# Lightning attention and SwiGLU on one core: the loads of two groups moved ahead of two transposes in the load queue

## The chip, the cores and the metric

The kernel runs on one core of a Trainium2 chip. The metric is device microseconds of one execution, from the chip's own clock. Beside it stands one execution taken by the hardware profiler, whose span runs from the first to the last instruction of the program.

## The reference

Linear attention with a decay per head is followed by a gated feed-forward layer. Inputs q, k and v have batch 4, 8 heads, 768 positions and 64 columns; everything is float32.

```python
for b in range(nb):                      # blocks of 64 positions
    intra = einsum('bhic,bhjc->bhij', qb, kb) * Dmask          # lam ** (i - j), i >= j
    intra = einsum('bhij,bhjd->bhid', intra, vb)
    inter = einsum('bhid,bhde->bhie', qb * lam_pow, kv_state)
    out[:, :, sl] = intra + inter
    kv_state = lam_block * kv_state + einsum('bhsd,bhse->bhde', kb * rev_pow, vb)
x = out.transpose(0, 2, 1, 3).reshape(3072, 512)
g = x @ w_gate                           # 512 x 1536
y = (g * sigmoid(g) * (x @ w_val)) @ w_out                     # 1536 x 512
```

## The kernel before

The 3072 rows are cut into 12 groups of 256 positions of one batch row, numbered 0 to 11. Two groups make one tile of the feed-forward layer, so there are six tiles, t = 0 to 5. The ninth and the tenth group have the numbers 8 and 9, and form tile 4.

Each group goes through the same stations:

- `load_group` (L255) issues its loads on SP's queue, through `load_fp32` (L101). From group 6 on (`NAT0`), k and q are each loaded in four pieces of 64 partitions (128 KB each), and v in two pieces of 128 partitions (256 KB each): ten DMA issues, L114, 1.5 MB.
- `cast_scaled` (L267) converts k to bf16 on ScalarE (L270), scales q on VectorE (L272) and then calls `dma_transpose` (L260), which issues one transposing DMA (L263) from the tile `qk` to the tile `qkt`, again on SP's queue. It waits for both conversions. In what follows, T6 is the transpose of group 6, and so on.
- `v_scale` (L247) writes the decayed v, on GpSimd or, for group 7, on VectorE.
- `attend` (L696) is the attention of group g and the start of group g + 1: the product of q with the state (`core_a`, L475), the state update's products of g + 1 (`upd_mm`, L396), its scores (`scores_n`, L364, the first to read `qkt` of g + 1), and then the product with v of group g (`core_b`, L488).

The feed-forward part of a tile runs over 12 columns of 128 (`ffn_fc`): four gate products (L530), Silu on ScalarE (L534), four value products (L546), and their product h on VectorE (L549). The output product of tiles 0 and 1 is `ffn_out` (L565), which copies to `osb` on ScalarE (L567) and stores through ScalarE's queue (L568). Later tiles use `out_units` (L639), with sums and differences of h made by `h_combo` (L611).

Nothing reorders the instructions: the schedule is written by hand. A list of steps, one for each tile and column, is walked at L957 to L971; `at(n, fn, ...)` hangs a call on step n, and calls on one step run in the order in which they were registered. Each engine and each queue executes its instructions in the order in which they are issued. SP's queue carries the loads and the transposes, so a transpose that waits for a conversion holds all loads behind it.

For t = 2 the loop at L931 registers these calls, among others: on step `sn[4]` `cast_scaled(7)` and then `load_group(8)`, on step `sn[8]` `cast_scaled(8)` and then `load_group(9)`. For t = 3 it is `cast_scaled(9)` and `load_group(10)` on `sn[0]`, `cast_scaled(10)` and `load_group(11)` on `sn[6]`. `attend(6)` hangs on step 7 of t = 2, `attend(7)` on its step 10, `attend(8)` on step 4 of t = 3.

The loads' buffers come from a pool of ten (`raw`, for k, q and the weights) and one of four (`v`).

Of the kernel before, what the change touches and what calls it, by code (L numbers as in the profile page):

```python
# [19 lines left out]
@with_exitstack  # L20
def kernel(
    ctx: ExitStack,
    tc: tile.TileContext,
    q: bass.AP,
    k: bass.AP,
    v: bass.AP,
    lam: bass.AP,
    moe_w_gate: bass.AP,
    moe_w_val: bass.AP,
    moe_w_out: bass.AP,  # L30
    out: bass.AP,
):
    nc = tc.nc
    with tc.manual_schedule():
        _body(ctx, tc, nc, q, k, v, lam, moe_w_gate, moe_w_val, moe_w_out, out)


def _body(ctx, tc, nc, q, k, v, lam, moe_w_gate, moe_w_val, moe_w_out, out):
# [9 lines left out]
    NG = NBLK * B // 2  # L48
# [787 lines left out]
    def step(t, fc, b0=0, b1=B):  # L836
        steps.append((t, fc, b0, b1))
        return len(steps) - 1

    def at(n, fn, *a):  # L840
        plan.setdefault(n, []).append((fn, a))
# [83 lines left out]
    for t in range(2, NG // 2):  # L925
        order = [c for j in range(FC // 4) for c in (2 * j, 2 * j + 1, FH + 2 * j, FH + 2 * j + 1)]
        sn = [step(t, fc, 2 if t == 2 and fc < NH else 0) for fc in (range(FC) if t == 2 else order)]
        if t == 2:
            at(sn[4], ahead, 6)
            at(sn[5], v_scale, 7, nc.vector)  # L930
        for j, g in ((4 if t == 2 else 0, 2 * t + 3), (8 if t == 2 else 6, 2 * t + 4)):  # L931
            if g < NG:
                at(sn[j], cast_scaled, g)
                if g + 1 < NG:
                    at(sn[j], load_group, g + 1)
                if g > 7:
                    at(sn[1 + j], v_scale, g, nc.gpsimd)
        if t + 1 < NG // 2:
            at(sn[7 if t == 2 else 4], attend, 2 * t + 2)
            if 2 * t + 4 < NG:  # L940
                at(sn[10], attend, 2 * t + 3)
            else:
                at(sn[9], core_a, 2 * t + 3)
                at(sn[10], core_b, 2 * t + 3)
        for n, o in zip((1, 5, 7, 9) if t == 2 else ({3: 11, 4: 7, 5: 5}[t],), outs):
            at(sn[n], *o)
        if t == 2:
            at(sn[7], h_combo, t, 0)
            at(sn[9], h_combo, t, 1)
            at(sn[10], wo_combo, 3)  # L950
        else:
            at(sn[3], h_combo, t, 0)
            at(sn[7], h_combo, t, 1)
        at(sn[11], h_combo, t, 2)
        outs = [(out_units, t)]
# [47 lines left out]
```

## Time and profile before

| what | value |
| --- | --- |
| median of 3 runs | 223.6 us (223.45 to 225.53) |
| profiled execution | 222.9 us, its span 221.2 us |
| TensorE busy | 215.3 us, 97% of the span |
| VectorE, ScalarE, GpSimd busy | 126.2, 111.6, 87.8 us |
| granted TensorE clock | 1.00 |
| traffic | 28.31 MB read, 6.29 MB written |

The span is divided among the engines by their busy time; they overlap. In the lists of the profile, a row of the timeline has the start, the duration, the engine, the line, the operation and the tiles, and at its end in brackets the idle time before it with what ended it. PE is TensorE, DVE VectorE, ACT ScalarE, POOL GpSimd; a small q after the name (SPq) stands for the queue on which an engine issues its DMAs. A row of the waits names who waited for what, the total in us, how often, and the longest.

### The profile page before, as it was taken

The numbers are of one execution on the slowest core, as the hardware profiler recorded it, in microseconds if no ns is written. First come the engines' busy times: TensorE is split into PE (matmuls) and PEld (weight loads), VectorE is DVE, ScalarE is ACT, GpSimd is POOL, SyncE is SP. The second block draws the span as 40 slices with busy tenths as digits, with TensorE's granted clock in tenths as the row PEclk, the third lists the DMA queues.
The fourth block names the chain that finished last, engine by engine and source line by source line (L and its number), as shares of the span: only waits on it lengthen the run. The fifth ranks groups of instructions, "written<-read, shape, count | busy, mean of one in ns | idle before, by whom it ended". The sixth has DMA issues, their size and how long they took to land.

```text
span 221.2 us, 6418 instructions
## 1 busy us (share of the span) xinstructions
PE 215.3 (97%) x2636; PEld 136.4 (62%) x2636; DVE 126.2 (57%) x227; ACT 111.6 (50%) x235; POOL 87.8 (40%) x131
## 2 busy tenths in 40 slices
PE   8999999999999999999999899999999999999994
PEld 4666455888886556454444446864578444884583
DVE  1674357476763692842487888548663456434650
ACT  6788587655544342546273545335633453333332
POOL 6685746927593040589684635330610000000000
PEclk9999999999999999999999999999999999999999
DMA  6999999999997989498578778645001300022013
GB/s 189 343 341 362 372 358 318 265 271 197 375 280 169 235 235 220 128 242 216 118 196 201 166 160 202 157 153 134 3 1 74 119 3 1 0 89 104 0 47 142
DMA packets 88318, 39.72 MB, mean 180 GB/s; under 512 B 57698, under 2 KB 83938, under 8 KB 88290
## 3 DMA queue, kind: packets, MB, share of 16 engines
q1 hardware_dynamic: 84210, 33.50, 58.1%
q10 hardware_dynamic: 4080, 5.83, 7.2%
q8 instruction: 20, 0.33, 0.6%
q14 instruction: 8, 0.07, 0.1%
HBM read 28.31 MB, written 6.29 MB: 156 GB/s over the span
## 4 chain that ended last, share of the span: by engine, by line
PE 95%; ACT 2%; issue 1%; DVE 1%
PE bank L530 28%; PE bank L546 28%; PE bank L639 17%; PE bank L565 10%; PE bank L488 2%; PE bank L475 2%; PE bank L338 1%; PE bank L301 1%; PE bank L396 1%; PE bank L138 1%; PE bank L364 1%; ACT qkt L303 1%; PE bank L179 1%; DVE h L549 1%; PE bank L173 0%
## 5 line engine op out<-in xcount | busy, mean ns | idle before, releaser
L549 DVE TENSOR_TENSOR h<-sil,bank 128x512 bf16<-128x512 bf16 (+1 forms) x91 | 51.2, 574 | 58.2 <-PE bank L546 34.0
L546 PE MATMUL bank<-xt,wv_sb 128*128 128x512 bf16 (+1 forms) x364 | 77.0, 335 | 0.3 <-DVE h L549 0.3
L530 PE MATMUL bank<-xt,wg_sb 128*128 128x512 bf16 (+1 forms) x364 | 77.2, 335 | 0.0
L534 ACT ACTIVATE sil<-bank 128x512 bf16<-128x512 f32 (+1 forms) x91 | 46.1, 512 | 45.9 <-PE bank L530 41.2
L546 PEld LDWEIGHTS <-wv_sb 128*128 128x128 bf16 x364 | 35.5, 98 | 27.2 <-issue 0.6
L530 PEld LDWEIGHTS <-wg_sb 128*128 128x128 bf16 x364 | 34.3, 98 | 25.1 <-DVE xt L500 0.2
L250 POOL TENSOR_TENSOR v_s<-v,dec 128x1024 bf16<-128x1024 f32 (+1 forms) x14 | 22.0, 1582 | 27.2 <-DMA v<-in_v_dram 27.0
L565 PE MATMUL bank<-wo_sb,h 128*128 128x512 bf16 x96 | 21.9, 379 | 0.0
L639 PEld LDWEIGHTS <-h 128*128 128x128 bf16 x192 | 18.8, 98 | 3.0
L345 DVE TENSOR_TENSOR ssb<-bank,causal 128x512 bf16<-128x512 f32 x24 | 15.5, 684 | 5.1 <-PE bank L338 5.0
L435 POOL TENSOR_TENSOR kvf<-kvs,ups 128x256 f32<-128x256 f32 x8 | 5.8, 727 | 29.2 <-ACT ups L418 26.6
L639 PE MATMUL bank<-wo_sb,h 128*128 128x256 bf16 x144 | 16.9, 273 | 0.0
L565 PEld LDWEIGHTS <-h 128*128 128x128 bf16 x96 | 9.1, 98 | 10.4
L639 PEld LDWEIGHTS <-hs 128*128 128x128 bf16 x144 | 14.1, 98 | 1.7
L500 ACT CAST xt<-bank 128x512 bf16<-128x512 f32 x19 | 11.6, 656 | 3.5 <-PE bank L488 2.6
L567 ACT COPY osb<-bank 128x512 f32<-128x512 f32 x8 | 4.7, 587 | 16.6 <-PE bank L565 16.6
L444 POOL CAST kvn<-kvf 64x256 bf16<-64x256 f32 x24 | 11.5, 478 | 1.5
L435 POOL TENSOR_TENSOR kvf<-kvf,ups 128x256 f32<-128x256 f32 x16 | 11.8, 736 | 0.6
L639 PE MATMUL bank<-wt,hs 128*128 128x256 bf16 x96 | 11.7, 273 | 0.0
L418 ACT COPY ups<-bank 128x256 f32<-128x256 f32 (+1 forms) x24 | 9.5, 451 | 1.5 <-PE bank L396 1.3
L270 ACT CAST qk<-kraw 128x1024 bf16<-128x1024 f32 x9 | 9.4, 1043 | 0.4 <-DMA kraw<-in_k_dram 0.4
L272 DVE TENSOR_TENSOR qk<-qraw,qdn 128x1024 bf16<-128x1024 f32 x6 | 8.0, 1328 | 2.7 <-DMA qraw<-in_q_dram 2.7
(89 smaller groups left out, 216.8 us busy)
## 6 DMA issues: line engine op xcount, KB each, us to landing
out_dram<-osb ACTq DMA_DIRECT2D x20, 256.0 KB, 2.7
v<-in_v_dram SPq DMA_DIRECT2D x18, 256.0 KB, 4.5
woraw<-in_moe_w_out_dram SPq DMA_DIRECT2D x6, 512.0 KB, 6.6
kraw<-in_k_dram SPq DMA_DIRECT2D x24, 128.0 KB, 3.7
qraw<-in_q_dram SPq DMA_DIRECT2D x24, 128.0 KB, 3.6
wraw<-in_moe_w_gate_dram SPq DMA_DIRECT2D x5, 512.0 KB, 7.3
wraw<-in_moe_w_val_dram SPq DMA_DIRECT2D x5, 512.0 KB, 6.6
kraw<-in_k_dram SPq DMA_DIRECT2D x4, 512.0 KB, 6.3
```

The lines of the kernel that those rows point to most:

```text
L250: eng.tensor_tensor(out=st[("vs", g)][:, h0:h1], in0=st[("v", g)][:, h0:h1].rearrange("p h (s d) -> p h s d", s=2), in1=vfac(g, h0, h1), o ...
L345: nc.vector.tensor_tensor(out=ssb[:, h2, 2 * c:2 * c + 2].rearrange("p a s n -> p a (s n)"), in0=sp[(c, h2)].rearrange("p (a x) -> p a x", ...
L418: nc.scalar.copy(out=u[:, 0:n], in_=up[r][:, 0:n])
L435: nc.gpsimd.tensor_tensor(out=o, in0=f, in1=u, op=ALU.add)
L444: nc.gpsimd.tensor_copy(out=o[64 - h2 * 64:128 - h2 * 64], in_=f[h2 * 64:h2 * 64 + 64])
L500: fns[r](out=xt[:, g % 2, :, r].rearrange("p h (m s) -> p h s m", s=2) if g < NAT0 else xt[:, g % 2, :, :, r * M:r * M + M], in_=op[r].rea ...
L530: nc.tensor.matmul(gp[:, 0:N], wg_sb[:, mc, fs], xt[:, b0 // 2:b1 // 2, mc].rearrange("p g b n -> p g (b n)"), start=(mc == 0), stop=(mc = ...
L534: nc.scalar.activation(sil[:, 0:N], gp[:, 0:N], AF.Silu)
L546: nc.tensor.matmul(vp[:, 0:N], wv_sb[:, mc, fs], xt[:, b0 // 2:b1 // 2, mc].rearrange("p g b n -> p g (b n)"), start=(mc == 0), stop=(mc = ...
L549: nc.vector.tensor_tensor(out=h_sb[:, fc % FH, b0:b1].rearrange("p b n -> p (b n)"), in0=sil[:, 0:N], in1=vp[:, 0:N], op=ALU.mult)
L565: nc.tensor.matmul(ps, st[("h", t, fc // FH)][:, fc % FH, b], wo_sb[:, fc, c0:c1], start=(fc == 0), stop=(fc == FC - 1))
L639: nc.tensor.matmul(o, lhs(f), rhs(f), start=(start and f == 0), stop=(f == FH - 1), skip_group_check=True)
```

## The change

The loads of groups 8 and 9 are taken out of the loop and hung on steps of their own in tile t = 2: k and q of group 8 on `sn[1]`, its v on `sn[4]`, k and q of group 9 on `sn[6]`, its v on `sn[8]`. They are registered before the loop, so on one step they come ahead of `cast_scaled`. The condition `g > 8` leaves the loop's own loads to groups 10 and 11.

```diff
         if t == 2:
+            at(sn[1], load_group, 8, "kq")
+            at(sn[4], load_group, 8, "v")
+            at(sn[6], load_group, 9, "kq")
+            at(sn[8], load_group, 9, "v")
             at(sn[4], ahead, 6)
             at(sn[5], v_scale, 7, nc.vector)
         for j, g in ((4 if t == 2 else 0, 2 * t + 3), (8 if t == 2 else 6, 2 * t + 4)):
             if g < NG:
                 at(sn[j], cast_scaled, g)
-                if g + 1 < NG:
+                if g + 1 < NG and g > 8:
                     at(sn[j], load_group, g + 1)
```

On SP's queue the order changes as follows (each load stands for its ten issues); the instructions of all other engines keep their order:

```
before:  T6  v7  T7  kqv8  T8  kqv9  T9  kqv10  T10  kqv11  T11
after:   T6  v7  kqv8  T7  kqv9  T8  T9  kqv10  T10  kqv11  T11
```

## The prediction

> **What bounds the kernel now.** I read the first part of the page, the waits of TensorE, its timeline around the moved loads, then the timeline of SP's queue, where the change is made.
>
> ```profile
> PE 215.3 (97%) x2636; PEld 136.4 (62%) x2636; DVE 126.2 (57%) x227; ACT 111.6 (50%) x235; POOL 87.8 (40%) x131
> ```
>
> TensorE is busy 97% of the span and stands for 95% of the chain that ended last. An earlier load gains only where TensorE itself waits for it, and a wait put in front of TensorE is paid in full. Its waits between 60 and 160 us:
>
> ```profile
> PE bank L364 <- DMA qkt<-qk: 0.5, 1, 0.5
> PE bank L546 <- DVE h L549: 0.3, 1, 0.3
> ```
>
> Both fall in one stretch. Its timeline there, with that of group 7 and of group 8 before it:
>
> ```profile
> 98.03 0.49 PE L396 MATMUL bank<-v_s,qk 64*64 64x64 bf16 x32
> 98.34 0.60 PE L364 MATMUL bank<-qkt 64*64 64x64 bf16 x32
> ...
> 109.92 0.42 PE L396 MATMUL bank<-v_s,qk 64*64 64x64 bf16 x24
> 110.35 0.45 PE L364 MATMUL bank<-qkt 64*64 64x64 bf16 x32
> 110.62 0.46 PE L488 MATMUL bank<-ssb,v_s 64*64 64x64 bf16 x32
> 111.01 1.04 PE L530 MATMUL bank<-xt,wg_sb 128*128 128x512 bf16 x4
> 111.89 1.03 PE L546 MATMUL bank<-xt,wv_sb 128*128 128x512 bf16 x4
> ...
> 121.75 0.42 PE L396 MATMUL bank<-v_s,qk 64*64 64x64 bf16 x24
> 122.67 0.49 PE L364 MATMUL bank<-qkt 64*64 64x64 bf16 x32 [0.50 <-DMA qkt<-qk]
> ...
> 123.37 1.04 PE L530 MATMUL bank<-xt,wg_sb 128*128 128x512 bf16 x4
> 124.69 1.02 PE L546 MATMUL bank<-xt,wv_sb 128*128 128x512 bf16 x4 [0.28 <-DVE h L549]
> ```
>
> The L364 rows are the scores of groups 7 (98.34), 8 (110.35) and 9 (122.67); each needs its group's transpose, T7, T8, T9. Only group 9's is late. SP's queue around them:
>
> ```profile
> 57.47 8.51 SPq L263 DMA_TRANSPOSE qkt<-qk  x1
> ...
> 79.05 2.79 SPq L114 DMA_DIRECT2D qraw<-in_q_dram  x4
> 82.01 3.61 SPq L263 DMA_TRANSPOSE qkt<-qk  x1
> 85.66 1.20 SPq L114 DMA_DIRECT2D v<-in_v_dram  x2
> 92.37 1.57 SPq L263 DMA_TRANSPOSE qkt<-qk  x1
> ```
>
> T6 starts at 82.01, T7 at 92.37. A transpose with nothing in flight ahead takes 1.57 to 1.65 us on the queue (T7 to T11). T6, right behind loads, took 3.61; that of group 5, behind 3 MB of w_out, 8.51. The reader should compare their ends with the last load ahead. The last q piece before T6 was issued at 81.18 and landed 4.70 later, 85.88: T6's issue ended at 85.62. The last w_out piece was issued at 56.80, landed 9.37 later, 66.17: that issue ended at 65.98. T4, issued at 46.51 for 5.79 us, ended at 52.30, and the load ahead of it landed at 52.40. So a transpose stays on SP's queue until about 0.2 us before the loads ahead have landed. It then lands about 2.1 us later (T6 at 87.67, T7 at 96.09).
>
> **What it takes away.** With q of group 9 loaded long before, the vector engine's scaling at L272 (117.47, idle 1.69 before it for that DMA) runs right after the h product that ends at 115.78, takes its 1.23, and T9 starts near 117.2, not 118.83. It lands near 121.0, ahead of 122.2. From L396 to L364 group 8 takes 0.43, group 9 0.92: 0.49 us go. From L530 to L546 it is 0.88 against 1.32: that 0.44 is the vector engine still behind after its wait (busy 3.93 of the 4.00 us from 121 to 125). Both: 0.93. If the vector engine stays behind, 0.49. I take 0.9, since 1.69 us of idle time in front of that backlog disappear. TensorE's other gaps in the stretch are nil, so no gain exceeds this. The 1.05 us that group 10's scaling waited at 129.63 go too, but T10 already lands at 134.71, as its scores begin: nothing.
>
> **What it adds: ten issues ahead of T7.** They can start when the second v piece of group 7 is issued, 86.86; their buffers are free, since the w_out pieces that lay in them were cast by 65.3. Eight k and q issues at 0.65 make 5.2, two v issues at 0.62 make 1.25: 93.3. In the built program each issue also waits for an earlier DMA on the same of eight completion semaphores; the second q piece waits for the first v piece of group 7 (85.66 plus 4.86, which its twin took: 90.5), which makes the end 93.9. T7 itself was ready at 92.3, when the scaling ended, so the issuing alone costs 1.6, and a T7 landing 3.7 later, 97.7, would still beat 98.34. What matters is when the second v piece of group 8 lands. The v of group 7 landed at 91.14 (86.28 plus 4.86); behind it lie 1.57 MB. One k or q piece per 0.65 us is 200 GB/s, the GB/s row of the DMA view shows about 250 where v pieces flow: 6.3 to 7.9 us, and a store of 256 KB issued at 95.03 lies within (0.7 us at the 360 GB/s that the row shows beside stores). That gives 97.4 to 99.7. The shortest landing of a v piece behind its own loads (3.7, group 9) from 93.3 gives 97.0. I take 225 GB/s, the middle: 98.1. T7's issue then ends at 97.9 and lands at 100.0; TensorE waits from 98.34: **1.7 us**, bounds 0.6 (97.0) and 3.2 (99.7). Behind the waiting L364 stand the attention product L488, the output product at 99.19 and all gate and value products, so it is all path.
>
> **Ten issues of group 9 ahead of T8: nothing.** SP is free at 97.9; ten issues with their semaphore waits (the third q piece for T7's landing, the v pieces for k pieces behind it) end near 104, the last landing 4.0 later, 107.8. T8 waits for the scaling that ended at 106.49, 1.7 later now: 108.3, issue end 109.9. The cover is 2.1 us. Were it gone, each us would be paid, since T8 lands at 110.36 (106.62 plus 1.64 plus 2.1) for scores at 110.35. T9 then stands directly behind T8. The loads of group 10 are issued earlier than 120.47, and everything after keeps its order. The stores on ScalarE's queue now wait for landings of v7, v8 and k9 on shared semaphores: 91.1, 98.1 and about 103.5, against their issues at 95.03, 102.60 and 108.64; so the Silu behind them is not held. GpSimd's scaling of v9 (idle 2.75 for its load) starts earlier; nobody waited for it.
>
> **Sum.** Minus 0.9, plus 1.7: plus 0.8. The profiled execution took 222.9 (span 221.2 and 1.7 around it), so 223.7; the median of the runs is 0.7 above that execution, so 224.4. Own range, from plus 0.6 minus 0.93 to plus 3.2 minus 0.49 with the far corner cut: 223.3 to 225.9.
>
> A rule speaks against the stall. The Trainium skill, "DMA: Bandwidth & Descriptors", section "Queues, rings and completion order", says that data descriptors carry no barrier and that a later one may finish before an earlier; its "Rules for kernel authors" add that a transpose beside ordinary DMAs needs nothing. By that T7 would land at 97.7, the stall would be 0 and the time 222.7; the three long issues above show a transpose held behind loads, so I go by them.
>
> **Rivals.**
> 1. *T7 is not held.* It lands 3.7 after 93.9, TensorE waits nowhere, only the gain stays: 223.6 minus 0.9, 222.7. For it: T7, T9, T10 and T11 land in 3.7 to 3.8. Against: those had nothing in flight ahead; the three that had were held. 0.12.
> 2. *Slower: the backlog drains badly.* Place: the load queue between 87 and 99, shared with the stores issued at 86.46 and 95.03. When v8 lands after 99.6, T7 lands after 101.5, the stall passes 3.1 and the net passes 2.2 us, one per cent; at 100.5 it is 4.1 minus 0.9: 226.8. For it: a q piece took 4.70 to land with a store beside it, and all of v7, k8, q8, v8 (2.1 MB) now follow T6 without a pause, while before the transfers were idle from 92 to 93.5. Against: 2.1 MB in the 12 us from 87.5 need only 175 GB/s. 0.16. The Trainium skill, "TensorE: Matmul & The Clock Gate", section "Why this matters for your kernels", warns that idle gaps above about 3 us halve the clock; the 0.50 us gap here left it at 1.00, and no run shows a longer one.
> 3. *The gain does not come.* T9 still follows a late scaling, because the vector engine's list is the limit: plus 1.7, 225.3. For it: the 3.93 busy of 4.00. Against: the 1.69 us wait in front of it. 0.10.
>
> My forecast has 0.62. Over and under one per cent (2.2 us), about what a measurement of this kernel can tell from no change: faster needs more than the 0.93 that TensorE lost, 0.02; slower is rival 2, 0.16; the rest, 0.82, lies within. The range goes from rival 1 to the start of rival 2: 222.6 to 226.1.
>
> **What would show it.** In SP's timeline ten issues stand between 85.7 and about 94, and T7's issue is 3 to 5 us long, ending just before v8 lands. TensorE has one new gap of about 1.7 us before the L364 near 98.3, for qkt, and those at 122.67 and 124.69 are gone. The scaling of groups 9 and 10 waits for no DMA. A T7 issue of 1.6 us would prove the holding wrong; a new gap before the scores of group 8 would prove the cover of T8 wrong; a wait of Silu behind a store would show a path that I priced at nothing.

## The result, and the profile after

The changed kernel is slower. Over 20 executions of each, its median is 228.2 us (225.6 to 230.3) against 223.8 us (222.9 to 226.2); the ratio is 1.015 (95% interval [1.012, 1.019]), about 3.4 us. This ratio and those below are of means, and leave out executions more than 1.5% above their kernel's fastest, so it stands below the 1.019 of the plain medians. The forecast was 224.4 us and no measurable change; what came is the slower rival, at the place that it named. The profiled execution took 229.2 us, its span 227.4 us, 6.2 more than before. It is one of the longer ones of its kernel, and that of before (222.9) one of the shorter, so the 6.2 us taken apart here are more than the usual difference.

From the page: the total, the busy time, and the row of TensorE and of its granted clock in 40 slices of 5.7 us.

```profile
span 227.4 us, 6411 instructions
...
PE 215.8 (95%) x2631; PEld 136.4 (60%) x2636; DVE 124.9 (55%) x227; ACT 111.5 (49%) x235; POOL 87.0 (38%) x131
...
PE   8889999999999999946999999999999999999994
...
PEclk9999999999999999995999999999999999999999
```

TensorE's work is the same; one hole has come, in slices 18 and 19, and the clock halves behind it. Its timeline there and at the next two groups:

```profile
98.45 0.49 PE L396 MATMUL bank<-v_s,qk 64*64 64x64 bf16 x32
103.74 0.64 PE L364 MATMUL bank<-qkt 64*64 64x64 bf16 x32 [4.80 <-DMA qkt<-qk]
...
105.14 4.11 PE L565 MATMUL bank<-wo_sb,h 128*128 128x512 bf16 x11 [0.34 <-issue]
109.09 1.03 PE L530 MATMUL bank<-xt,wg_sb 128*128 128x512 bf16 x4
...
118.19 1.04 PE L530 MATMUL bank<-xt,wg_sb 128*128 128x512 bf16 x4
...
130.01 1.04 PE L530 MATMUL bank<-xt,wg_sb 128*128 128x512 bf16 x4
130.89 0.81 PE L546 MATMUL bank<-xt,wv_sb 128*128 128x512 bf16 x3
```

The same stretch before, behind the scores at 98.34:

```profile
99.19 2.76 PE L565 MATMUL bank<-wo_sb,h 128*128 128x512 bf16 x12
101.78 1.03 PE L530 MATMUL bank<-xt,wg_sb 128*128 128x512 bf16 x4
```

The scores of group 7 wait 4.80 us for T7. The two waits of before, for T9 and for h at group 9, are gone, and the scores of group 8 do not wait. The windows of TensorE give busy time by engine, then the granted clock, the DMA share and the GB/s:

```profile
98.40:103.80 5.40, 0.60 (x65) 0.49 (x56) 0.65 (x1) 1.23 (x3) 4.29 (x9) 0.79 1.06 218
103.80:108.40 4.60, 4.26 (x72) 2.22 (x74) 0.69 (x1) 1.07 (x2) 4.00 (x5) 0.51 0.77 173
```

From about 101.5 to 108.3 the clock is half: the output product at 105.14 takes 4.11 us where it took 2.76. So the 6.2 us of span can be put together from the timelines of both:

| stretch | before | after | difference |
| --- | --- | --- | --- |
| start of L396 ahead of group 7's scores | 98.03 | 98.45 | +0.4 |
| L396 to L364: the wait for T7 | 0.31 | 5.29 | +5.0 |
| L364 of group 7 to the first L530: the half clock | 3.44 | 5.35 | +1.9 |
| first L530 after group 8's scores to that after group 9's | 12.36 | 11.82 | -0.5 |
| that L530 to its L546 | 1.32 | 0.88 | -0.4 |

The rest is -0.1. The gain that was forecast is in the last two rows; the stall was three times the forecast, and a second price came with it. On SP's queue:

```profile
84.13 2.89 SPq L263 DMA_TRANSPOSE qkt<-qk  x1
87.07 1.34 SPq L114 DMA_DIRECT2D v<-in_v_dram  x2
88.52 3.34 SPq L114 DMA_DIRECT2D kraw<-in_k_dram  x4
91.97 3.82 SPq L114 DMA_DIRECT2D qraw<-in_q_dram  x4
95.83 1.54 SPq L114 DMA_DIRECT2D v<-in_v_dram  x2
97.54 4.18 SPq L263 DMA_TRANSPOSE qkt<-qk  x1
...
113.65 12.88 SPq L263 DMA_TRANSPOSE qkt<-qk  x2
```

T7 leaves at 97.54, 5.2 us later than before, and stays 4.18 us, until 101.72; the last v piece of group 8 landed at 101.75. T7's own landing is not recorded; its scores start at 103.74, 2.0 us after its issue. The last row is two transposes and the idle time between them: T8 from 113.65 for 1.61 us, T9 from 124.23 for 2.30 us.

The wait differs between executions. A second profiled execution of the changed kernel, taken beside the experiments (`after_again`), shows where else it can go.

> The changed kernel once more, for a second profile of the same order: T7's issue again between 3 and 4.5 us long, the wait before the scores of group 7 between 2.5 and 5 us, no wait before the scores of groups 8 and 9. If the wait passes about 3 us the clock is halved for some us behind it, otherwise not.

It took 230.4 us (span 228.7). T7's issue was as long as expected, 3.98 us; the waits were not as expected. TensorE waited 1.25 us for T7 at 102.39 and then 2.61 us for T8:

```profile
116.83 0.45 PE L364 MATMUL bank<-qkt 64*64 64x64 bf16 x32 [2.61 <-DMA qkt<-qk]
```

Here T7 started earlier (95.79) and TensorE arrived 2.2 us later, probably because a piece of half clock from 15.7 to 19.1 us, long before the change, had delayed it (3.4 us at half speed are 1.7 us). T8's issue took a clean 1.61 us, from 111.46, and yet it landed only at 116.79, beside a store issued at 112.52.

The clock sorts the 20 executions. A mean clock of 0.992 over 226 us is 3.6 us at half speed, 0.985 is 6.8 us.

| mean granted clock | executions | time, us |
| --- | --- | --- |
| 0.999 | 2 | 225.6, 225.8 |
| 0.990 to 0.992 | 10 | 226.0 to 229.2, median 227.6 |
| 0.984 to 0.985 | 8 | 228.4 to 230.3, median 229.0 |

Of 38 executions of the kernel before, taken beside the experiments, five show 0.992 and all others 0.997 or more. Not every such piece comes from the wait for T7 (`after_again` had one at 15.7 us), but 18 of 20 against five of 38 is the change's doing; the two executions without it lost some 1.9 us (225.7 against 223.8).

### The profile page after: what moved, and what is told of

Same layout as the page of the kernel before. It is cut to its first block, busy times and chain, and to the rows that moved or that the text cites. A ratio compares the mean times of both kernels' runs of the same rounds, so it can differ in the third digit from the quotient of the medians.

```text
span 227.4 us, 6411 instructions
## 1 busy us (share of the span) xinstructions
PE 215.8 (95%) x2631; PEld 136.4 (60%) x2636; DVE 124.9 (55%) x227; ACT 111.5 (49%) x235; POOL 87.0 (38%) x131
## 4 chain that ended last, share of the span: by engine, by line
PE 71%; SPq 8%; DMA 8%; issue 5%; POOL 4%; ACT 1%; DVE 0%; POOLq 0%
PE bank L530 23%; PE bank L546 23%; PE bank L639 16%; SPq L114 3%; SPq L107 3%; PE bank L565 3%; DMA wraw<-in_moe_w_val_dram 3%; DMA qkt<-qk 3%; DMA v<-in_v_dram 2%; SPq L225 2%; PE bank L488 2%; POOL v_s L250 2%; PE bank L475 1%; POOL kvf L435 1%; POOL kvn L444 1%
## 5 line engine op out<-in xcount | busy, mean ns | idle before, releaser
L530 PE MATMUL bank<-xt,wg_sb 128*128 128x512 bf16 (+1 forms) x364 | 77.2, 335 | 0.0
L546 PE MATMUL bank<-xt,wv_sb 128*128 128x512 bf16 (+1 forms) x364 | 77.1, 335 | 0.1
L546 PEld LDWEIGHTS <-wv_sb 128*128 128x128 bf16 x364 | 35.5, 98 | 27.1 <-DVE wv_sb L821 0.6
L530 PEld LDWEIGHTS <-wg_sb 128*128 128x128 bf16 x364 | 34.3, 98 | 25.1 <-DVE xt L500 0.2
L250 POOL TENSOR_TENSOR v_s<-v,dec 128x1024 bf16<-128x1024 f32 (+1 forms) x14 | 21.5, 1542 | 24.9 <-PE bank L565 10.5
L565 PE MATMUL bank<-wo_sb,h 128*128 128x512 bf16 x91 | 23.0, 400 | 0.5 <-issue 0.3
L639 PEld LDWEIGHTS <-h 128*128 128x128 bf16 x192 | 18.8, 98 | 3.0
L565 PEld LDWEIGHTS <-h 128*128 128x128 bf16 x96 | 9.6, 103 | 11.7 <-issue 2.4
L444 POOL CAST kvn<-kvf 64x256 bf16<-64x256 f32 x24 | 12.4, 516 | 1.5
L369 DVE TENSOR_TENSOR ssb<-bank,causaln 128x512 bf16<-128x512 f32 x12 | 8.2, 686 | 5.8 <-PE bank L364 5.7
```

Of the source, the lines that this page charges most:

```text
L250: eng.tensor_tensor(out=st[("vs", g)][:, h0:h1], in0=st[("v", g)][:, h0:h1].rearrange("p h (s d) -> p h s d", s=2), in1=vfac(g, h0, h1), o ...
L444: nc.gpsimd.tensor_copy(out=o[64 - h2 * 64:128 - h2 * 64], in_=f[h2 * 64:h2 * 64 + 64])
L530: nc.tensor.matmul(gp[:, 0:N], wg_sb[:, mc, fs], xt[:, b0 // 2:b1 // 2, mc].rearrange("p g b n -> p g (b n)"), start=(mc == 0), stop=(mc = ...
L546: nc.tensor.matmul(vp[:, 0:N], wv_sb[:, mc, fs], xt[:, b0 // 2:b1 // 2, mc].rearrange("p g b n -> p g (b n)"), start=(mc == 0), stop=(mc = ...
L565: nc.tensor.matmul(ps, st[("h", t, fc // FH)][:, fc % FH, b], wo_sb[:, fc, c0:c1], start=(fc == 0), stop=(fc == FC - 1))
L639: nc.tensor.matmul(o, lhs(f), rhs(f), start=(start and f == 0), stop=(f == FH - 1), skip_group_check=True)
```

## The experiments

The theory before them (A): a transpose stays on SP's queue until the loads ahead have landed; T7 is late by that, and the half clock adds to it. The rivals are told in each expectation. An edit is against the changed kernel, unless the text names the kernel before.

**Only group 9 ahead** (`g9_only`): group 8's loads stay behind T7, as before.

```diff
-            at(sn[1], load_group, 8, "kq")
-            at(sn[4], load_group, 8, "v")
...
-                if g + 1 < NG and g > 8:
+                if g + 1 < NG and g != 8:
```

> Only the ten loads of group 9 go ahead of T8; those of group 8 stay behind T7, as before the change. Theory A (the loss is T7, held on SP's queue until the v pieces of group 8 have landed, and the half clock that follows; the gain of 0.93 at the scores of group 9 is real): no stall before the scores of group 7, no late scaling of q of group 9, the two gaps near 122 gone, about 0.9 us below the kernel before, ratio 0.996. Rival B (the loads of group 9 ahead of T8 cost too, because T8 lands just as its scores begin): a gap before the scores of group 8, ratio 1.000 or above.

Ratio 1.032 [1.029, 1.035]: the half that I held harmless costs more than the whole. SP's queue, and the scores of group 8:

```profile
102.93 3.11 SPq L114 DMA_DIRECT2D kraw<-in_k_dram  x4
106.85 2.63 SPq L114 DMA_DIRECT2D qraw<-in_q_dram  x4
109.52 3.83 SPq L114 DMA_DIRECT2D v<-in_v_dram  x2
113.52 15.70 SPq L263 DMA_TRANSPOSE qkt<-qk  x2
```

```profile
117.83 0.64 PE L364 MATMUL bank<-qkt 64*64 64x64 bf16 x32 [6.66 <-DMA qkt<-qk]
```

Group 9's ten issues now follow group 8's without a pause and keep T8 off the queue until 113.52, where it was ready at 107.3. Some 3 us of that are one wait: the second v piece was issued only at 112.98, when a store of 109.47, the last DMA on the same completion semaphore, had landed (112.97). Ten loads in front of the next transpose do the same kind of damage. In the profile of the changed kernel, where group 8's were issued ahead of T7, group 9's ended at 109.05 and T8 was not late.

**Only group 8 ahead** (`g8_only`).

```diff
-            at(sn[6], load_group, 9, "kq")
-            at(sn[8], load_group, 9, "v")
...
-                if g + 1 < NG and g > 8:
+                if g + 1 < NG and g != 7:
```

> Only the ten loads of group 8 go ahead of T7; those of group 9 stay behind T8. Theory A: the whole loss and none of the gain: a stall of 3.5 to 5 us before the scores of group 7, the clock halved for some us after it, and about 0.9 us above the changed kernel, ratio 1.019. Rival B: clearly below the changed kernel's 1.015.

Ratio 1.010 [1.004, 1.016]; the interval overlaps that of the whole change, and the 1.019 forecast for the loss without the gain lies above it. The wait for T7 is there, 3.70 us (T7 on the queue from 97.10, 3.98 us long), with 6.8 us of half clock behind it; T8 is not late. The loss at group 7 is group 8's.

**v of group 8 behind T7** (`v8_behind`): eight pieces ahead of T7 instead of ten.

```diff
-            at(sn[4], load_group, 8, "v")
...
                 at(sn[j], cast_scaled, g)
+                if g == 7:
+                    at(sn[j], load_group, 8, "v")
```

> As the changed kernel, but the two v pieces of group 8 are issued behind T7; its eight k and q pieces stay ahead. Theory A: T7 starts about 1.7 us sooner and is held until the last q piece has landed, so its issue is still 3 us or longer, and it lands about 2.5 us sooner than in the changed kernel: a stall of 2 to 2.5 us, little or no half clock, ratio 1.004 to 1.008. Rival C (T7 is late only by the issues ahead of it, it is not held): its issue takes 1.6 us, the stall is about 0.8 us, ratio 0.999 to 1.001.

Ratio 1.013 [1.008, 1.019], from four executions that spread from 227.2 to 233.6 us; 1.004 to 1.008 was forecast. T7 left at 95.22, stayed 3.31 us, and TensorE waited 2.05 us at 100.61, as expected. Not expected was a second wait at group 8: the v pieces and group 9's ten were still in front of T8.

```profile
114.67 0.45 PE L364 MATMUL bank<-qkt 64*64 64x64 bf16 x32 [2.23 <-DMA qkt<-qk]
```

The clock stayed at 1.00 through both. The span, 225.7 us, is 1.7 us shorter than that of the changed kernel's profile, although the two waits add up to 4.28 us.

**TensorE kept busy during the wait** (`fill`). Fourteen products of 512 columns on a constant go into the bank of the scores before group 7's; the scores overwrite them. Nothing else changes.

```diff
         sp = [bank() for _ in range(2)]
+        warm_into(sp[0], 14 if g == 7 else 0, 512)
```

> As the changed kernel, with 14 products of 512 columns on constants (3.0 us, results overwritten) put just before the scores of group 7, where TensorE waits for T7. Theory A (part of the loss is the half clock after the stall): T7 lands as late as before, but the products keep TensorE busy for 3.0 us of the wait, the granted clock stays 1.00, and the time falls to that of the stall alone, ratio 1.008 to 1.010. If the half clock is not part of the loss: ratio 1.015 or above, as the changed kernel.

Ratio 1.007 [1.004, 1.010], about 0.8% below the changed kernel, with 3.23 us of useless work added. TensorE's timeline (the line of the scores is one higher in this kernel), and its window from 102 us on, with the clock in the third column from the end:

```profile
98.73 3.23 PE L179 MATMUL bank<-const-bfloat16-1.0 128*128 128x512 bf16 x14
101.90 0.45 PE L365 MATMUL bank<-qkt 64*64 64x64 bf16 x32
```

```profile
102.00:110.00 8.00, 8.00 (x99) 3.95 (x99) 3.53 (x5) 3.78 (x6) 5.51 (x9) 1.00 0.85 204
```

T7 landed at 101.11 (on the queue from 95.17 to 99.09), 5.0 us later than before, though 2.6 us sooner than in the profile of the changed kernel, since T6 had left sooner (81.37). The clock is whole; nine of its ten executions have a mean clock of 0.998 or more. The two kernels issue the same DMAs in the same order, and their intervals do not meet, so the half clock is a part of the loss by itself, about 1.9 us (0.85% of 223.8). The Trainium skill, "TensorE: Matmul & The Clock Gate", section "Why this matters for your kernels", asks for no idle gaps above about 3 us. The profiles agree above that: gaps of 3.70 us (`g8_only`), 4.80 us (the changed kernel) and 6.66 us (`g9_only`) brought 6.8 us of half clock each. Below it they do not draw a line: gaps of 2.05 and 2.23 us (`v8_behind`) brought none, the 2.61 us of `after_again` brought 3.4, and in `attend_late` the clock was halved at 114.53, behind a gap of 2.16 us (112.00 to 114.16) and before the next one began.

**Only k of group 9 ahead of T8** (`k9_ahead`): the kernel before, with four issues moved into the time in which SP's queue waited for T8.

```diff
             at(sn[5], v_scale, 7, nc.vector)
+            at(sn[7], load_fp32, 9, nc.sync, k, "kraw")
...
-                    at(sn[j], load_group, g + 1)
+                    at(sn[j], load_group, g + 1, "qv" if g == 8 else "kqv")
```

> The kernel before, with only the four k pieces of group 9 issued ahead of T8; its q and v pieces stay behind. SP's queue was idle from 101.7 to 106.6 there, and four issues need 2.7 us. Theory A (a transpose is held until the loads ahead have landed): the pieces land near 107.8, before the 1.6 us of T8's own issue are over, so T8 is not held; q of group 9 lands about 2.7 us sooner, its scaling does not wait, T9 is not late, and the gaps of 0.93 near 122 go: ratio 0.996. Rival B: the gap before the scores of group 9 is chance of one execution: ratio 1.000 within 0.002. Rival C (any load ahead of T8 delays it): a gap before the scores of group 8, ratio 1.003 or above.

Ratio 0.992 [0.988, 0.995], median 222.3 us: faster than both kernels. SP's queue:

```profile
102.86 2.97 SPq L114 DMA_DIRECT2D kraw<-in_k_dram  x4
106.90 1.59 SPq L263 DMA_TRANSPOSE qkt<-qk  x1
108.54 2.77 SPq L114 DMA_DIRECT2D qraw<-in_q_dram  x4
...
117.35 2.50 SPq L263 DMA_TRANSPOSE qkt<-qk  x1
```

T8 is hardly moved (106.90) and not held; q of group 9 follows it in time, VectorE's scaling waits for nothing, T9 leaves at 117.35 and no product of TensorE waits for a DMA. T9 stayed 2.50 us, although the last load had landed at 117.51. The gain of 1.8 us is twice what I forecast for it. The profiled executions of before lie at the lower end of their kind (222.9 and 222.7 against medians of 223.6 to 224.3); where the others lose the rest, no profile shows.

**k and q of group 9 ahead of T8** (`kq9_ahead`): eight issues instead of four.

```diff
+            at(sn[7], load_group, 9, "kq")
...
-                    at(sn[j], load_group, g + 1)
+                    at(sn[j], load_group, g + 1, "v" if g == 8 else "kqv")
```

> The kernel before, with the eight k and q pieces of group 9 ahead of T8, its v pieces behind: four pieces more than in the run with the k pieces alone, whose last k piece landed at 108.59, just under the end of T8's issue. Theory A (held until the loads ahead have landed): the eight issues end near 108.6, so T8 starts 1.7 us late; the last q piece lands near 112, T8's issue takes about 3 us and ends with it, and TensorE waits 3 to 3.5 us before the scores of group 8; ratio 1.004 to 1.012. Rival (T8 is late only by the issues ahead): T8's issue takes 1.6 us, the wait is about 1.8 us, ratio 0.998 to 1.002.

Ratio 1.030 [1.026, 1.034]; both sides had forecast far less. T8 left at 108.94 and stayed 3.00 us, the length that theory A forecast, but landed only at 117.23, 5.3 us after its issue ended; a store issued at 109.12 landed at 115.02. The length proves little here: T9, with nothing in flight ahead of it, stayed 2.90 us.

```profile
108.94 3.00 SPq L263 DMA_TRANSPOSE qkt<-qk  x1
115.04 1.47 SPq L114 DMA_DIRECT2D v<-in_v_dram  x2
126.23 2.90 SPq L263 DMA_TRANSPOSE qkt<-qk  x1
```

```profile
117.27 0.64 PE L364 MATMUL bank<-qkt 64*64 64x64 bf16 x32 [6.45 <-DMA qkt<-qk]
```

The dose ahead of T8 therefore reads: four pieces 0.992, eight 1.030, ten 1.032. In `k9_ahead` the four issues ended at 105.83, before T8 was ready (106.8); here the eight ended at 108.78, after it was (107.0). So the step lies where the issues outgrow the pause ahead of the transpose, though half of the wait of 6.45 us is the late landing (5.3 us after the issue instead of about 2).

**v of group 8 on GpSimd's queue** (`v8_pool`), one step earlier: if only loads of its own queue hold a transpose, T7 is held less.

```diff
-    def load_group(g, parts="kqv"):
+    def load_group(g, parts="kqv", eng=nc.sync):
...
-                load_fp32(g, nc.sync, src, what)
+                load_fp32(g, eng, src, what)
...
+            at(sn[0], load_group, 8, "v", nc.gpsimd)
...
-            at(sn[4], load_group, 8, "v")
```

> As the changed kernel, but the two v pieces of group 8 are issued by GpSimd on its own queue one step earlier; k and q of group 8 stay ahead of T7 on SP's queue. If a transpose is held only by loads of its own queue, T7's issue ends when the last q piece of group 8 lands, whenever the v pieces land: stall 1.5 to 2.5 us, T8 not late, ratio 1.002 to 1.007. If it is held by all loads in flight, its issue ends with the v pieces too, should they land later than the q pieces: stall 4 us or more, ratio 1.012 or above.

Ratio 1.018 [1.010, 1.027], from four executions of 227.3 to 235.3 us. Neither side had it. T6 was caught: it stayed 5.48 us, and the scores of group 6 waited 1.13 us. T7 stayed only 2.96 us but landed 4.6 us after that, beside a store issued at 97.31, and TensorE waited 3.79 us. T6's issue ended at 88.89, between the last landing of its own queue (88.36) and that of GpSimd's (89.11), so the question stayed open here.

**T7 on ScalarE's queue** (`t7_act`) puts the question again.

```diff
-        nc.sync.dma_start(out=tt.rearrange("p a s h n -> p (a s h) n"),
+        (nc.scalar if g == 7 else nc.sync).dma_start(out=tt.rearrange("p a s h n -> p (a s h) n"),
```

> As the changed kernel, with all loads where they are, but T7 alone is issued on ScalarE's queue, right after the conversion of k of group 7, near 92.7. If a transpose is held only by loads of the queue it is issued on: its issue takes about 1.6 us there, T7 lands at 97 to 98.5, before its scores, the stall is below 0.5 us and the ratio 0.993 to 1.000. If it is held by every load in flight, whichever queue it came from: the issue lasts until the loads of group 8 have landed, 5 us or more, ScalarE and its Silu stand still meanwhile, ratio 1.015 or above.

Ratio 1.015 [1.011, 1.019], no better than the change. ScalarE's queue, then TensorE:

```profile
92.62 2.44 ACTq L263 DMA_TRANSPOSE qkt<-qk  x1
```

```profile
115.22 0.65 PE L364 MATMUL bank<-qkt 64*64 64x64 bf16 x32 [3.88 <-DMA qkt<-qk]
```

The issue ends at 95.06, while q and v of group 8 land on SP's queue until 98.9 and 101.0: it is not held for them, in this one profile. But it lands only at 99.47, 4.4 us later, with those loads and a store issued at 96.20 in flight beside it. The wait for T7 is nearly gone (0.68). It comes back at T8: the next k piece of group 9, on SP's queue, shares a completion semaphore with T7 and could be issued only at 99.49, T8 left at 107.58, was held 4.00 us, and landed at 115.18.

**TensorE's need for T7 moved back** (`attend_late`): the attention of group 6 and the scores of group 7 stand one step later.

```diff
-            at(sn[7 if t == 2 else 4], attend, 2 * t + 2)
+            at(sn[8 if t == 2 else 4], attend, 2 * t + 2)
```

> As the changed kernel, but the attention of group 6, with the scores of group 7, is hung one step later, so TensorE needs T7 about 4.3 us later (one column of gate and value products, 1.73, and one output product, 2.59). Theory A (the loss is the lateness of T7 against its need, and SP's queue then has no time left before T8): the stall before the scores of group 7 falls below 1 us and the clock stays 1.00, but T8 is held by the loads of group 9 and its scores wait 1 to 3 us: ratio 1.003 to 1.010. Rival (T7 alone is late): no stall before the scores of group 8, ratio 0.996 to 1.002.

Ratio 1.018 [1.010, 1.027], above what either side forecast. The scores of group 7, at 104.50, find T7 landed at 103.96 and do not wait. The lateness is handed to group 8:

```profile
114.16 0.44 PE L396 MATMUL bank<-v_s,qk 64*64 64x64 bf16 x24 [2.16 <-POOL v_s L250]
117.79 0.64 PE L364 MATMUL bank<-qkt 64*64 64x64 bf16 x32 [3.19 <-DMA qkt<-qk]
```

T8 left at 109.78, was held 4.10 us and landed at 117.74. The 2.16 us for GpSimd's v, which now comes late as well, I had not foreseen, nor the half clock from 114.53 to 121.36.

**The kernel before, profiled again** (`before_again`).

> The kernel before, unchanged, for a second profile: if the 0.50 and 0.44 us near the scores of group 9 belong to the schedule, they are there again, each within 0.3 us; if they are chance, the scores of group 9 follow without a gap. A transpose with no load in flight ahead of it takes 1.6 us on SP's queue again, T6 behind its loads over 2.5.

222.7 us, span 221.0. The wait for T9 was 0.26 us and L530 to L546 behind it 1.13: the same two losses, half as large.

## Why the prediction failed, step by step

- **The gain at group 9** (0.93 us): right between these two profiles, where its parts measured 0.54 and 0.44 us. Its usual size is not settled: `before_again` lost only 0.51 us there, and `k9_ahead`, which moves only four of these loads, gained 1.8.
- **A transpose is held until the loads ahead of it have landed** (T7's issue of 3 to 5 us, landing about 2.1 us after it): right for T7. It stayed 4.18 us, and its issue ended within 0.2 us of the landing of the last load ahead in the changed kernel, `v8_behind`, `fill` and `attend_late`; `t7_act` shows, in one profile, that loads of another queue do not hold it so. The rule weighed in the prediction, that a transpose beside ordinary DMAs needs nothing, may hold for what is computed; for the time, these rows speak against it. But the 1.57 to 1.65 us taken for a transpose with nothing ahead are not the whole of it: T9 directly behind a T8 that had long landed stayed 1.56 us in `fill` and `v8_behind`, but 2.30 in the changed kernel and up to 3.02 in `t7_act`. Something besides loads can lengthen the issue, and no run shows what.
- **"Eight k and q issues at 0.65 make 5.2 ... which makes the end 93.9": this step failed.** From the first v piece of group 7 to T7's start I had 85.66 to 93.9, 8.2 us; the profile has 10.5 (87.07 to 97.54), and four others with the same ten pieces ahead of T7 have 9.9 (`g8_only`), 10.2 (`after_again`), 10.4 (`fill`) and 11.3 (`attend_late`). Single issues took 0.58 to 1.78 us. I had added 0.6 us for one wait on a shared completion semaphore, but that is not what made them long: for eight of group 8's ten issues the trace has the landing of the DMA that last used the semaphore, and each time it lies before the issue began. The longest, 1.78 us from 91.97, used the semaphore of T6, which had landed at 89.04. Why issues take so long there stays open. The trace of before had the row: k and q of group 7, issued beside stores from 73.75 on, took 8.1 us for eight issues, 1.0 us each.

```profile
73.75 5.26 SPq L114 DMA_DIRECT2D kraw<-in_k_dram  x4
```

- **The start of that row was taken as fixed.** T6 left at 82.01 in the profile of before, at 81.4 to 84.2 in the others; here 84.13, so the v pieces behind it began 1.4 us late. Together 1.4 and 2.1 (the 2.3 above without the 0.2 us between the last issue and T7) are the 3.5 us by which the last issue ended late (97.37, forecast 93.9); the landing behind it took 4.4 for the forecast 4.2, and so T7 landed at 103.7 instead of 100.0.
- **The half clock** was cited under the slower rival, as a threshold that no run showed, and stood in no sum. It cost 1.9 us in the profile, and `fill` measures about the same.
- **"Ten issues of group 9 ahead of T8: nothing"**: right in the profile of the changed kernel, wrong as a reason. T8 was not held there and landed at 117.33, just ahead of its scores (117.41), but `after_again` waited 2.61 us for T8, and in `g9_only`, `v8_behind`, `attend_late` and `t7_act` T8 was late by 2.2 to 6.7 us when T7 was less late or not at all. I had read that T8 has no slack and gave it no chance of its own.
- **The slower rival** had place and sign. Its price, 4.1 less 0.9, is close to the measured 3.4, but that is luck: the transfers did not drain badly. The issues came late, and the half clock cost the rest.

Besides the two above, two things stay open. That a transpose beside a store lands late is seen in rows only (below), without a cause. And no profile shows a kernel of the changed order at 225.6 us, so what its best executions lose is known by `fill` alone.

## What to carry to other kernels

A queue that carries both loads and transposes has room only in its pauses: here, moving loads ahead of T8 paid while they fitted into the pause (four pieces, 0.992) and cost a stall beyond it (eight, 1.030). Before moving a step past others on a queue, list for each transpose when it must land and what slack it has, and price the issues by the slowest row that had stores beside it. A stall of TensorE near 3 us is priced with the half clock behind it; here waits of 2.1 to 2.6 us went both ways.

## What was not expected of the hardware

- A transpose whose issue ends while a store of 256 KB has some 2 us or more to go mostly lands late: 2.6 to 5.3 us after that end (T7 or T8 in `after_again`, `v8_behind`, `v8_pool`, `kq9_ahead` and `t7_act`), against 2.0 to 2.3 us where no store was (T8 and T9 in the changed kernel 2.07 and 2.00, T9 in `kq9_ahead` 2.28; T7 in `g8_only` 2.0, whose store had landed at 99.95 against the issue's end at 101.08). In `v8_pool` T7 landed 0.32 us behind the store, in `after_again` T8 0.43 us behind it. T6 in the changed kernel, with a store issued 0.13 us before its issue ended, landed 2.0 us after it, so the order of the two may count. No run isolates this.
- The half clock came 2.0 us (`g8_only`) to 5.2 us (`kq9_ahead`) after the gap began, and lasted 6.8 us behind each of the six gaps of 3.70 to 6.66 us, whatever its length. In `g8_only` TensorE was at work again 1.7 us after the clock had halved, and ran 5.1 us more at half speed. A long gap is not needed: in `after_again` the half clock from 15.70 to 19.11 followed two gaps of 0.74 and 0.55 us (13.70 to 15.21), where TensorE was busy 1.88 of the 3.42 us before.
- Lateness crosses queues through the shared completion semaphores: T7 on ScalarE's queue held SP's next load until 99.49, and a store held SP's v piece until 115.04 in `kq9_ahead`.
